# Attention and two feed-forward blocks on one core: conversion temporaries moved to the place of the last value weights, mixes of the second unit moved to the value products, first operations reordered

## The chip, the cores and the metric

The kernel runs on one core of one Trainium2 chip. The metric is device time in microseconds (us) of one execution; the median of the runs counts. Engines are named as the profile names them: PE is TensorE (PEld its weight loads), DVE is VectorE, ACT is ScalarE, POOL is GpSimd, SP issues the DMAs.

## The reference, cut to what matters

Attention with a causal mask and a bias from a running sum, then a block that mixes each row with the row before it, then a gated block. B, H, S, D are 4, 8, 576, 64; the model width is 512, the inner width 1024.

```
def _attn_ref(q, k, v, s):
    scores = q @ k^T / 8
    cum = cumsum(max(s, 0))
    scores = where(causal, -1e9, scores + minimum(-(cum_i - cum_j), 0))
    return softmax(scores) @ v
...
def _moe_ref(x, mu_k, mu_r, w_k, w_v, w_r):
    xk = mu_k * x + (1.0 - mu_k) * x_prev
    xr = mu_r * x + (1.0 - mu_r) * x_prev
    k = np.maximum(xk @ w_k, 0.0)
    v = k * k @ w_v
    r = 1.0 / (1.0 + np.exp(-(xr @ w_r)))
    return r * v
...
def _moe2_ref(x, w_in, g_ln, w_sg, b_sg, w_out):
    h = gelu(x @ w_in); u, v = halves of h
    v_s = w_sg @ layernorm(v) + b_sg
    return x + (u * v_s) @ w_out
```

## The kernel before, in words

**Numbers in two parts.** The weights of the first block are 64-bit words. `load_words` brings 128 x 512 of them (512 KB) by one DMA; `convert` makes two fp32r halves of them: ACT takes an absolute value of the high words (L110), DVE does two scalar operations (L114, L115) and two joins with the words (L116, L117) in a temporary `cvt`, ACT casts it to the first half (L70), DVE subtracts to the second (L73). There are 20 such conversions: 0 to 7 of wk, 8 to 11 of wr, 12 to 19 of wv; `conversions` is a generator that loads AHEAD = 5 ahead. The two temporaries are the halves of one tile `temps`, tag "rt" of the pool `mwork` (L750). A matmul in two parts is three products: high by high, low by high, high by low (`mm3_steps`, L661).

**Attention.** `attend()` is a generator over 20 jobs; each is a pair of heads. Batch 0 has two jobs a pair: jobs 0 to 3 with the row blocks 0 to 2, jobs 4 to 7 with the row blocks 3 and 4. Batches 1 to 3 have one job a pair (jobs 8 to 19, five blocks). Each step issues the scores of a block for one head (L344, from job 6 on L346 and L347), the fold with mask and minimum on DVE (L361), the exponential on ACT (L387), and part of the job before: transposes (L422, L526), values (L426, L430, L511). From job 8 on the reciprocals of the sums go through memory (`reciprocals`, `spread`), and POOL scales the result xt (L492). `prepare` splits the operands of a job (L327 to L333) and, from job 6 on, loads its bias rows from `gate_d`, which is written once at the start (L298).

**First block.** `moe1()` goes through 8 units, halves of a batch (288 rows). A unit has 8 groups of products with wk (f, 12 matmuls each), 4 groups with wr (m, 12 each), 4 groups with wv (m, 24 each): 240 matmuls. The wk groups end in `kh` and `kl`, the wr groups in a tanh into `rt` (L635, tile tag "rt" in `mwork`), the wv groups in a multiplication with rt on DVE (L647). Ahead of a unit stand its 8 mixes, `mix(u, j, c)`: ACT (L594), DVE (L600), a cast on ACT (L70) and a subtraction on POOL (L73, xl). A unit may be mixed only when its attention is done: `need(u)` issues attention steps until `done[0] > u`. For odd units, `late`, the mixes of the next unit are issued beside the wv groups as soon as done allows, else behind them; for even ones, unit 0 among them, `mix(u + 1, 1, m)` stands behind wr group m and `mix(u + 1, 0, m)` behind wv group m.

**Order.** The order of issue is written by hand in the loop from L805 on: after every second matmul of the first block `due` rises by 2 / Q0 (10) while done is at most 1, by 2 / Q1 (6) while it is at most 2, and by 2 / Q2 (8) after that, and one attention step is issued for each whole one. done is 1 after job 3, 2 after job 7, 4 after the scaling of job 11, 6 and 8 after those of jobs 15 and 19. Products of the first block are tied to follow the latest attention matmul on PE (L663). Within that, a scheduler orders each engine's instructions by priority (`tc.cur_priority`; a smaller number goes first: the first operations -100000, attention -1000, conversions -500, mixes -500). A tile of a new pool that lies on the place of closed pools waits until all of these have been used.

**The start.** s is loaded, cut at zero (L264), summed up by a scan (L266) and copied into the operand rows of job 0 (L269 to L272). The rest of the operand rows is filled by memsets (`rest`). POOL makes the identity and the mask (L249 to L260); mask0 is a copy with one corner set (L262, L263). `gt` is made from `cur` and written to `gate_d`. The tiles zer, cum, cur and gt are in the pool `cum`; it is closed at L299, and the pools opened after it (`xtp` with the tiles xt, `w1b` with wv, `mwork` with rt, xf, kh, kl, kf) take up the room behind it. mu is loaded at L304, after that, and mu1 made from it on POOL (L306). 14 matmuls of 512 columns without use warm up PE (L243).

Of the kernel before, what the change touches and what calls it, by code (L numbers as in the profile page):

```python
# [31 lines left out]
WARM = 14  # L32
# [3 lines left out]
L0, GATE = 0, 1  # L36
GC, LC = 0, 2
XT = 0
# [3 lines left out]
PACE = 3  # L42
N0 = 8
# [8 lines left out]
def block_kernel(ctx: ExitStack, tc: tile.TileContext, qkv, vb, s, w_r, w_k, w_v, mu, w_in, w_out, w_sgT, g_ln, b_sg, out):  # L52
# [184 lines left out]
    if WARM:

        ones = cp.tile([P, 512], BF16, name="ones")
        nc.vector.memset(ones, 1.0)  # L240
        pm = ps_m.tile([P, 512], F32, tag="m", name="warm")
        for _ in range(WARM):
            nc.tensor.matmul(pm, ones[:, 0:P], ones, start=True, stop=True)  # L243
# [29 lines left out]
    tc.cur_priority += FIRST - SECOND  # L273
    cur = cp.tile([48, S], F32, name="cur")
# [33 lines left out]
    xtp = ctx.enter_context(tc.tile_pool(name="xtp", bufs=2))  # L308
    w1b = tc.tile_pool(name="w1b", bufs=1)
    w1bp = w1b.__enter__()  # L310
    wv = Weight(w1bp, "wv", w_v)
# [438 lines left out]
    temps = mw.tile([P, 2, 512], F32, tag="rt", name="cvt")  # L750
# [282 lines left out]
```

## Time and profile before

| | |
|---|---|
| median of 3 runs | 714.64 us (714.37 to 714.86) |
| the profiled execution's own time | 712.34 us |
| its span, first to last instruction | 710.5 us |
| mean granted TensorE clock | 0.964 |
| PE busy | 670.2 us (94%) |
| DVE busy | 510.2 us (72%) |
| ACT busy | 407.8 us (57%) |
| POOL busy | 231.4 us (33%) |
| DMA | 67.48 MB, 95 GB/s in the mean |

One execution of the program is recorded. Busy is the time in which an engine executes; idle time of an engine that isn't the bottleneck costs nothing. The granted clock is 1.00 at 2.4 GHz and 0.50 at 1.2 GHz. A row of a timeline has the start, the duration, the engine, the line of the code, the operation with the tile written and those read, the number of merged instructions, and in brackets the engine's idle time before it with what ended it.

### The profile page before, as it was taken

What the parts mean: (1) busy time and instruction counts of PE and PEld (TensorE: products, weight loads), DVE (VectorE), ACT (ScalarE), POOL (GpSimd) and SP (SyncE); (2) the same over time, 40 slices, a digit from 0 to 9 for tenths busy, and PEclk for the clock granted to TensorE, in tenths of its full rate; (3) what the DMA queues carried; (4) which work ended last, traced back from release to release, by engine and by line L of the source; (5) the groups of instructions that cost most, each with busy time, mean ns of one, the idle gap of its engine ahead of it and who ended that gap; (6) DMA issues with size and microseconds to landing.
All of it is one profiled execution on the core that took longest, in us unless ns stands there. A gap on an engine that the chain in (4) does not pass through costs nothing.

```text
span 710.5 us, 12931 instructions
## 1 busy us (share of the span) xinstructions
PE 670.2 (94%) x4594; PEld 630.0 (89%) x4594; DVE 510.2 (72%) x1225; ACT 407.8 (57%) x978; POOL 231.4 (33%) x234
## 2 busy tenths in 40 slices
PE   6879979998999979999989999999999999999998
PEld 3657879987999969998989999999998998998998
DVE  8869998877878688779678598852946664664643
ACT  5759776877988867797777453633433133133120
POOL 7013553546655763576463073030000000000000
PEclk8779976999999999999999999999999999999999
DMA  9884542345244332424200630004230400300101
GB/s 242 238 253 145 155 123 56 95 125 159 73 128 141 89 107 57 143 85 119 89 22 21 204 131 29 6 18 142 78 117 3 131 3 5 129 1 5 63 1 68
DMA packets 39832, 67.48 MB, mean 95 GB/s; under 512 B 6908, under 2 KB 23400, under 8 KB 39736
## 3 DMA queue, kind: packets, MB, share of 16 engines
q1 hardware_dynamic: 39768, 66.66, 31.5%
q8 instruction: 36, 0.59, 0.3%
q14 instruction: 28, 0.23, 0.1%
HBM read 51.85 MB, written 10.19 MB: 87 GB/s over the span
## 4 chain that ended last, share of the span: by engine, by line
PE 71%; ACT 10%; DVE 10%; issue 3%; DMA 3%; POOL 1%; SPq 1%; DVEq 0%; ACTq 0%; POOLq 0%
PE m L661 25%; PE pu L674 7%; PE po L674 7%; PE av L511 3%; PE t L526 3%; PE pg L912 2%; PE pg L913 2%; ACT pr L387 2%; PE pg L911 2%; PE s L346 2%; PE av L430 2%; PE pv L848 2%; PE pv L849 2%; PE pv L850 2%; PE s L347 2%
## 5 line engine op out<-in xcount | busy, mean ns | idle before, releaser
L387 ACT ACTIVATE pr<-pr,nm 128x448 f32<-128x448 f32 (+4 forms) x144 | 85.3, 593 | 19.0 <-DVE nm L361 15.4
L73 POOL TENSOR_TENSOR xl<-xf,xh 128x288 fp32r<-128x288 f32 x64 | 69.0, 1091 | 79.5 <-ACT xh L70 40.5
L661 PE MATMUL m<-xh,wk 128*128 128x288 f32 x512 | 82.6, 300 | 0.0
L661 PE MATMUL m<-kh,wv 128*128 128x288 f32 x512 | 79.8, 297 | 0.0
L361 DVE CUSTOM_DVE_ANT_0 pr<-s,mask 128x288 f32<-128x288 f32 (+4 forms) x144 | 64.0, 454 | 15.6 <-PE t L526 6.4
L661 PEld LDWEIGHTS m<-xh,wk 128*128 128x128 f32 x512 | 73.0, 191 | 0.8
L661 PEld LDWEIGHTS m<-kh,wv 128*128 128x128 f32 x512 | 71.7, 188 | 0.5
L346 PE MATMUL s<-qk 128*128 128x288 f32 (+4 forms) x144 | 47.4, 330 | 12.2 <-DVE nh L361 7.7
L600 DVE SCALAR_TENSOR_TENSOR xf<-xt,mu_sb,xf 128x288 f32<-128x288 f32 x64 | 43.8, 688 | 12.4 <-ACT xf L594 12.2
L70 ACT CAST xh<-xf 128x288 fp32r<-128x288 f32 (+1 forms) x80 | 36.3, 482 | 24.2 <-DVE xf L600 13.5
L530 DVE TENSOR_TENSOR ptl<-t,pth 128x512 fp32r<-128x512 f32 (+1 forms) x72 | 44.1, 617 | 6.3 <-ACT pth L529 5.9
L661 PE MATMUL m<-xl,wk 128*128 128x288 f32 x256 | 48.1, 303 | 0.0
L594 ACT ACTIVATE xf<-xt,mu 128x288 f32<-128x288 f32 x64 | 33.9, 536 | 24.4 <-POOL xl L73 17.8
L529 ACT CAST pth<-t 128x512 fp32r<-128x512 f32 (+1 forms) x72 | 37.8, 532 | 15.6 <-PE t L526 15.0
L73 POOL TENSOR_TENSOR qk<-qld,qk 64x576 fp32r<-64x576 f32 (+1 forms) x28 | 38.9, 1389 | 20.3 <-DVE qk L70 4.3
L347 PE MATMUL s<-qk 128*128 128x288 f32 (+4 forms) x144 | 44.7, 313 | 0.0
L661 PE MATMUL m<-kl,wv 128*128 128x288 f32 x256 | 44.1, 299 | 0.0
L622 ACT ACTIVATE kf<-m 128x288 f32<-128x288 f32 x64 | 25.9, 410 | 30.6 <-PE m L661 28.9
L346 PEld LDWEIGHTS s<-qk 128*128 128x128 f32 x144 | 28.0, 194 | 16.4 <-DVE nh L361 9.1
L661 PE MATMUL m<-xh,wr 128*128 128x288 f32 x256 | 41.0, 301 | 1.3 <-ACT rt L635 1.0
L674 PE MATMUL pu<-xh,wi 128*128 128x288 f32 x256 | 40.6, 295 | 0.2 <-ACT ut L874 0.2
L70 ACT CAST gh<-gf 128x288 fp32r<-128x288 f32 x32 | 13.9, 435 | 46.0 <-DVE gf L918 46.0
(296 smaller groups left out, 1861.4 us busy)
## 6 DMA issues: line engine op xcount, KB each, us to landing
kld<-qkv SPq DMA_DIRECT2D x28, 288.0 KB
qld<-qkv SPq DMA_DIRECT2D x24, 288.0 KB
x_d<-rt SPq DMA_DIRECT2D x8, 576.0 KB
xf<-x_d SPq DMA_DIRECT2D x8, 576.0 KB
outT<-ot SPq DMA_DIRECT2D x32, 144.0 KB
vld<-qkv SPq DMA_DIRECT2D x24, 160.0 KB
qk<-qk SPq DMA_DIRECT2D x24, 144.0 KB
rb<-rd SPq DMA_DIRECT2D x24, 128.0 KB
```

Of the source, the lines that this page charges most:

```text
L70: nc.scalar.copy(dst, src) if eng == "A" else nc.vector.tensor_copy(dst, src)
L73: (nc.gpsimd if pick(engines) == "P" else nc.vector).tensor_tensor(dst, a, b.bitcast(F32), ALU.subtract)
L346: nc.tensor.matmul(dst, qk[0][:, 0, qs], qk[0][:, 1, ks], start=True, stop=False)
L347: issued[0] = nc.tensor.matmul(dst, qk[1][:, 0, qs], qk[1][:, 1, ks], start=False, stop=True)
L361: nc.vector.tensor_tensor_reduce(out=dst, in0=src, in1=msk, scale=-0.125, scalar=first, op0=ALU.add, op1=ALU.min, accum_out=acc)
L387: i = nc.scalar.activation(dst, dst, AF.Exp, bias=nm[:, col : col + 1], scale=-1.0, accum_out=w.sm[:, col : col + 1])
L529: nc.scalar.copy(pth[:, cols], bank[:, 0:o])
L530: nc.vector.tensor_tensor(ptl[:, cols], bank[:, 0:o], pth[:, cols].bitcast(F32), ALU.subtract)
L594: nc.scalar.mul(xf, xp, mu1[:, j, c : c + 1])
L600: nc.vector.scalar_tensor_tensor(xf, xc, mu_sb[:, j, c : c + 1], xf, ALU.mult, ALU.add)
L661: i = nc.tensor.matmul(dst, w(x, c, m), xx[:, c], start=(n + c == 0), stop=(n == 2 and c == w.nk - 1))
L674: nc.tensor.matmul(dst, w(x, c, m), xx[:, c], start=(n + c == 0), stop=(n == 2 and c == w.nk - 1))
```

## The change

- The temporaries of the conversions are a tile in the place (tag) of the last value weight, wv70, in the pool `w1b`; the last two conversions use a tile `more` of the tag "rb" instead. The last value weight is loaded behind conversion 17.
- L0 is 1: unit 0 counts as late, so the mixes of unit 1 are issued beside or behind the wv groups of unit 0.
- `xtp` and `w1b` are opened before the pool `cum`, so only `mwork` lies on its place.
- mu is loaded with the first loads.
- An exponential of one column stands at the beginning of ACT.
- The low memsets of operand 0's middle part are on DVE; the mask is made before the identity, and mask0 after the first operations, at lower priority.
- The work on gt has priority +300 instead of -1000.
- The warm-up is 18 matmuls of 384 columns; its tile is in the pool `const`.

```
-WARM = 14
+WARM = 18
-L0, GATE = 0, 1
+L0, GATE = 1, 1
+GT = 300
...
-    def conversions(parts, temps, loaded=0):
+    def conversions(parts, temps, loaded=0, last=None):
+        n = len(parts) if last is None else len(parts) - 1
         for i in range(loaded, len(parts) + AHEAD):
-            if i < len(parts):
+            if i < n:
                 load_words(*parts[i], after=temps(i - AHEAD - 1) if i > AHEAD else None)
             if i >= AHEAD:
                 convert(*parts[i - AHEAD], temps(i - AHEAD))
+                if i - AHEAD == last:
+                    load_words(*parts[-1])
                 yield
...
-    def rest(x, a, b, eng):
+    def rest(x, a, b, eng, low):
         eng.memset(qk[x][D:, 0, a:b], 8.0)
-        nc.gpsimd.memset(qk[x][D:, 1, a:b], 0.0)
-        nc.gpsimd.memset(qk[x][D : D + 1, 1, a:b], -8.0)
+        low.memset(qk[x][D:, 1, a:b], 0.0)
+        low.memset(qk[x][D : D + 1, 1, a:b], -8.0)
...
     cur_d = dram.tile([48, S], F32, name="cur_d")
+    mu_sb = const.tile([P, 2, 4], F32, name="mu_sb")
+    nc.sync.dma_start(mu_sb, mu)
+    xtp = ctx.enter_context(tc.tile_pool(name="xtp", bufs=2))
+    w1b = tc.tile_pool(name="w1b", bufs=1)
+    w1bp = w1b.__enter__()
+    wv = Weight(w1bp, "wv", w_v)
     cpool = tc.tile_pool(name="cum", bufs=1)
     cp = cpool.__enter__()
...
+    ones = const.tile([P, 384], BF16, name="ones")
+    nc.vector.memset(ones, 1.0)
+    idle = ps_m.tile([P, 512], F32, tag="m", name="warm")
+    for _ in range(WARM):
+        nc.tensor.matmul(idle[:, 0:384], ones[:, 0:P], ones, start=True, stop=True)
+    first = const.tile([P, 1], F32, name="first")
+    nc.scalar.activation(first, ones[:, 0:1], AF.Exp)
...
-    rest(0, S - KN[2], S + KN[2], nc.vector)
-    rest(1, S - KN[2], S + KN[2], nc.vector)
-    ident = const.tile([P, P], F32, name="ident")
-    make_identity(nc, ident)
+    rest(0, S - KN[2], S + KN[2], nc.vector, nc.vector)
     mask = const.tile([P, 2 * MD + P], F32, tag="mask", name="mask")
...
-    mask0 = const.tile([P, P], F32, name="mask0")
-    nc.vector.tensor_copy(mask0, mask[:, MD : MD + P])
-    nc.vector.memset(mask0[D:, 0:D], 8.0 * NEG)
+    ident = const.tile([P, P], F32, name="ident")
+    make_identity(nc, ident)
+    rest(1, S - KN[2], S + KN[2], nc.vector, nc.gpsimd)
...
     tc.cur_priority += FIRST - SECOND
+    mask0 = const.tile([P, P], F32, name="mask0")
+    nc.vector.tensor_copy(mask0, mask[:, MD : MD + P])
+    nc.vector.memset(mask0[D:, 0:D], 8.0 * NEG)
...
-    tc.cur_priority += SECOND - THIRD
+    tc.cur_priority += SECOND + GT
     gt = cp.tile([48, 2, 4, S], F32R, name="gt")
...
     cpool.__exit__(None, None, None)
-    tc.cur_priority += THIRD
-    mu_sb = const.tile([P, 2, 4], F32, name="mu_sb")
-    nc.sync.dma_start(mu_sb, mu)
+    tc.cur_priority -= GT
...
-    temps = mw.tile([P, 2, 512], F32, tag="rt", name="cvt")
+    temps = w1bp.tile([P, 2, 512], F32, tag="wv70", name="cvt")
+    more = ap.tile([P, S], F32, tag="rb", name="cvt")
     def temp(i):
-        return temps[:, i % 2]
+        return temps[:, i % 2] if i < 18 else more[:, 0:512]
     cvs = conversions(
         [(wk, c, n) for n in range(2) for c in range(4)] + [(wr, c, 0) for c in range(4)] + [(wv, c, 0) for c in range(8)],
         temp,
         loaded=AHEAD,
+        last=17,
     )
```

## Rows read from the trace of the kernel before

**Rows 1.** The page: busy time of PE, and its clock in 40 slices

```profile
PE 670.2 (94%) x4594; PEld 630.0 (89%) x4594; DVE 510.2 (72%) x1225; ACT 407.8 (57%) x978; POOL 231.4 (33%) x234
...
PEclk8779976999999999999999999999999999999999
```

**Rows 2.** Stretches: their length, busy us (count) of PE, PEld, DVE, ACT, POOL; clock, DMA

```profile
0.00:54.80 54.80, 40.13 (x175) 28.89 (x175) 43.39 (x139) 35.21 (x101) 18.09 (x50) 0.78 0.88 243
94.40:121.70 27.30, 22.09 (x112) 20.72 (x113) 25.64 (x54) 18.21 (x41) 11.74 (x10) 0.62 0.31 85
94.40:123.65 29.25, 24.04 (x127) 22.67 (x128) 27.27 (x58) 19.68 (x45) 12.62 (x11) 0.65 0.29 79
159.20:223.00 63.80, 61.43 (x450) 58.20 (x450) 51.06 (x133) 52.18 (x138) 37.52 (x31) 1.00 0.40 115
```

**Rows 3.** Timeline of the start (start, duration, engine, line, operation, tiles, idle before)

```profile
5.36 1.28 ACT L270 ACT_TABLE_LOAD   x1 [5.36 <-DVE cum L266]
6.34 1.58 POOL L159 MEMSET qk<- 1x640 f32 x2
7.40 1.10 PE L344 MATMUL s<-qk 128*128 128x320 f32 x4 [0.62 <-POOL qk L159]
8.25 0.30 POOL L252 TENSOR_SCALAR_AFFINE_SELECT mask<-mask 128x128 f32<-128x128 f32 x1
10.98 0.21 DVE L262 COPY mask<-mask 128x128 f32<-128x128 f32 x1
11.11 0.47 DVE L361 CUSTOM_DVE_ANT_0 pr<-s,mask 128x320 f32<-128x320 f32 x1
```

**Rows 4.** Timeline, 36 to 43 us

```profile
36.22 0.43 SPq L304 DMA_DIRECT2D mu_sb<-mu  x1
40.43 0.20 POOL L306 TENSOR_SCALAR mu<-mu_sb 128x8 f32<-128x8 f32 x1 [9.16 <-DMA mu_sb<-mu]
42.23 0.45 PE L440 MATMUL t<-ident,pr 128*128 128x128 f32 x1 [4.08 <-ACT p L424]
```

**Rows 5.** Timeline, 93 to 125 us

```profile
93.70 0.69 PE L661 MATMUL m<-xl,wr 128*128 128x288 f32 x4
121.74 1.24 PE L661 MATMUL m<-xh,wr 128*128 128x288 f32 x8
122.70 0.95 DVE L73 TENSOR_TENSOR wv<-cvt,wv 128x512 fp32r<-128x512 f32 x1 [0.32 <-ACT wv L70]
124.19 0.70 ACT L635 ACTIVATE rt<-m 128x288 f32<-128x288 f32 x2
```

**Rows 6.** The chain that ended last: products in a row (start, us)

```profile
393.48 9.90 PE m L661 x76
```

**Rows 7.** Conversions, 94.4 to 123.65: busy us of DVE, ACT; then min/median/max ns

```profile
94.40:123.65 29.25, 16.84 (x23) 5.28 (x9) 0.65 0.29 79
...
L73 DVE TENSOR_TENSOR wv<-cvt,wv x5: 644/686/1747, 100.7 to 122.7; 128x512 fp32r<-128x512 f32 x5
L115 DVE TENSOR_SCALAR cvt<-cvt x4: 421/425/428, 97.3 to 117.8; 128x512 int32<-128x512 int32 x4
```

**Rows 8.** Timeline of DVE: a mix

```profile
249.61 3.01 DVE L600 SCALAR_TENSOR_TENSOR xf<-xt,mu_sb,xf 128x288 f32<-128x288 f32 x1
```

**Rows 9.** Timeline: two loads and their first users; the gate DMAs, the xt memsets

```profile
3.91 0.43 SPq L101 DMA_DIRECT2D wk10w<-w_k  x1
10.74 0.67 ACT L110 ACTIVATE cvt<-wk10w 128x512 f32<-128x512 f32 x1 [0.75 <-DMA wk10w<-w_k]
13.71 0.97 SPq L298 DMA_DIRECT2D gate_d<-gt x2
21.72 0.31 POOL L716 MEMSET xt<- 128x1 f32 x8 [3.42 <-DMA qk<-cur_d]
```

**Rows 10.** Timeline, change from unit 1 to unit 2

```profile
215.39 1.43 POOL L492 TENSOR_TENSOR xt<-xt,rb 128x576 f32<-128x576 f32 x1 [0.88 <-DMA rb<-rd]
221.56 0.30 PE L661 MATMUL m<-xh,wk 128*128 128x288 f32 x1
```

More of the change, by code (lines that the diff above doesn't have):

```diff
@@ L35 @@
 U0 = 2
-L0, GATE = 0, 1
+L0, GATE = 1, 1
 GC, LC = 0, 2
-XT = 0
 E1, ND, SECOND, THIRD = 2, 2, 5000, 1000
@@ L234, in block_kernel @@
     cur_d = dram.tile([48, S], F32, name="cur_d")
+    mu_sb = const.tile([P, 2, 4], F32, name="mu_sb")
[4 more added lines that the diff above has]
+    wv = Weight(w1bp, "wv", w_v)
     cpool = tc.tile_pool(name="cum", bufs=1)
     cp = cpool.__enter__()
[L237 to L243, printed above, removed]
+    ones = const.tile([P, 384], BF16, name="ones")
[5 more added lines that the diff above has]
+    nc.scalar.activation(first, ones[:, 0:1], AF.Exp)
     zer = cp.tile([48, S], F32, name="zer")
     nc.gpsimd.memset(zer, 0.0)
-    rest(0, S - KN[2], S + KN[2], nc.vector)
-    rest(1, S - KN[2], S + KN[2], nc.vector)
-    ident = const.tile([P, P], F32, name="ident")
-    make_identity(nc, ident)
+    rest(0, S - KN[2], S + KN[2], nc.vector, nc.vector)
     mask = const.tile([P, 2 * MD + P], F32, tag="mask", name="mask")
@@ L281, in block_kernel @@
         for a, b in ((0, S - KN[2]), (S + KN[2], 2 * S)):
-            rest(x, a, b, nc.gpsimd)
+            rest(x, a, b, nc.gpsimd, nc.gpsimd)
     for c in range(max(1, E1), AHEAD):
         load_words(wk, c % 4, c // 4, after=cur)
-    tc.cur_priority += SECOND - THIRD
+    tc.cur_priority += SECOND + GT
     gt = cp.tile([48, 2, 4, S], F32R, name="gt")
@@ L299, in block_kernel @@
     cpool.__exit__(None, None, None)
-    tc.cur_priority += THIRD
-    mu_sb = const.tile([P, 2, 4], F32, name="mu_sb")
-    nc.sync.dma_start(mu_sb, mu)
+    tc.cur_priority -= GT
     mu1 = const.tile([P, 2, 4], F32, name="mu1")
     nc.gpsimd.tensor_scalar(mu1, mu_sb, -1.0, 1.0, ALU.mult, ALU.add)
[L308 to L311, printed above, removed]
     mwork = tc.tile_pool(name="mwork", bufs=1)
@@ L749, in block_kernel @@
     att = attend()
-    temps = mw.tile([P, 2, 512], F32, tag="rt", name="cvt")
-    more = [ap.tile([P, S], F32, tag=t, name="cvt") for t in ("rb",)] if XT else []
+    temps = w1bp.tile([P, 2, 512], F32, tag="wv70", name="cvt")
+    more = ap.tile([P, S], F32, tag="rb", name="cvt")
     def temp(i):
-        if i < XT:
-            return more[0][:, 0:512] if i % 3 == 2 else temps[:, i % 3]
-        return temps[:, i % 2]
+        return temps[:, i % 2] if i < 18 else more[:, 0:512]
     cvs = conversions(
```

## The prediction

> **What bounds the kernel now.** I read the page's first part, then the stretches, then the timeline at each stretch where TensorE loses time. Over the whole span TensorE is the bound: 94% busy, so some 40 us idle in all, and a change can only give back idle time or time at the lower clock [rows 1]. That time is not spread evenly: the string of granted clocks falls below 9 only in the first seven slices, that is before 125 us [rows 1], and from 159 to 223 us TensorE is busy 61.43 of 63.8 us at full clock [rows 2]. Ahead of that, VectorE (DVE) is the bound: busy 43.39 of the first 54.8 us, and 27.27 of the 29.25 us in which the last weight conversions run [rows 2]. So the early part is to be read as a row of DVE work with a few holes, and what counts is how early that row ends and what TensorE finds to do meanwhile.
>
> Three places stand out.
> 1. The start. The first scores begin at 7.40 and the mask is ready at 8.55 (8.25 + 0.30), but the first fold starts at 11.11, behind the copy of mask0 at 10.98 on the in-order DVE [rows 3].
> 2. A hole at 36 to 42 us. The load of mu_sb is issued only at 36.22. POOL idles 9.16 us for it and does the scaling of pr only behind it; ACT and TensorE follow, TensorE having idled 4.08 us [rows 4].
> 3. The stage of the r products of unit 0 (wr; a unit is half a batch). Its first group ends at 94.39; the next begins at 121.74, and its evacuation, the tanh into rt, comes at 124.19, after the last conversion's subtraction (122.70 + 0.95) [rows 5]. Two causes are written in the code: rt and the conversion temporaries have one tag, hence one place, and the mixes of unit 1 ahead of wr group 1 call need(1), which issues the attention up to job 8 in one go, ahead of further wr products.
>
> **The change, part by part.** The sum is made against the profiled execution, 712.34 us (span 710.5); the median shown is 714.64, 2.3 higher, and I carry the difference over to it.
>
> *Start (T1).* On POOL the mask goes ahead of ident; mask0's copy and memset leave the head of the queue; one Exp at the beginning draws the table load (1.28 us at 5.36, on the way to the first scores [rows 3]) into time in which ACT is idle (ACT's first work is at that load); the two low memsets of operand 0 go from POOL to DVE, whose gaps hide them (11.4 us idle before 54.8 [rows 2]); without that cover they cost DVE what they cost POOL, 0.79 us for the row of -8 [rows 3]. If the fold starts when its mask is ready, 11.11 - 8.55 = 2.6 us. Below: 0, if DVE's other early work merely changes places; above 3.9, with the table load counted too. I take 2.6, the row of the mask being the nearest. The warm-up becomes 18 x 384 instead of 14 x 512 columns (6912 for 7168): nothing.
>
> *The hole (T2).* mu_sb is now loaded with the first loads, one issue of 0.43 us on SP; what is queued behind it there are operands of job 1, not needed before the first job is through. POOL's mu1 then no longer stands before pr. I take TensorE's own wait, 4.1 us; 0 if DVE's row swallows it, 5.5 if the lower clock behind the hole goes as well.
>
> *Temporaries and mixes (T3).* In 94.4 to 121.7 TensorE is busy 22.09 us at a mean clock of 0.62 [rows 2]. With the 5.2 idle us at either clock the work is 11.7 to 14.3 us at full clock; I take the middle, 13.0, so 14.3 of 27.3 us are lost. That work is some 8 attention steps (done reaches 2 at step 18, ten to eleven are issued before): 1.6 us each. After the change wr's three other groups no longer wait for rt, nor for the burst: 36 products at 9.90/76 = 0.13 us [rows 6] are 4.7 us, and at one step per ten products 3.6 steps (5.9 us) lie among them: 10.6 us of TensorE work. But DVE still has the conversions, 16.84 us [rows 7], and its other 10.4 us (27.27 - 16.84) shrink only to 3.6/8, 4.7. So 21.5 us pass in which TensorE works 10.6: 10.9 us are still lost, 3.4 us are gained. Beside it, the conversions are longer than they need be: clean, these 23 instructions would take 8 x 0.43 and 15 x 0.69 (the subtraction's median, taken for the joins too), 13.8 us [rows 7]; the excess of 3.0 us comes while POOL subtracts (1.75 instead of 0.69 at worst). About half of POOL's subtractions leave the stretch: 1.5 us. T3 = 4.9; below 0, above 14.3 (all that is lost).
>
> The Trainium skill, page "SBUF — State Buffer", section "Who interferes with whom", says that a DVE instruction with two SBUF inputs contends with a GpSimd instruction that reads SBUF, one blocking the other. The trace agrees: a mix's multiply-add takes 3.01 us at 249.61 [rows 8]. It speaks against the change: the mixes' POOL subtractions don't vanish, they come where folds and the same multiply-adds run. By the rule alone T3 would be 3.4 and the time 707.5.
>
> *Given back (T4).* Without the burst attention is behind. Counting the issues at one step per 10, 6 and 8 products: before, unit 0 ends at step 40 and unit 1 at 80, and done reaches 4 at step 76, just in time for unit 2's mixes. After, done reaches 2 halfway through the second of unit 0's four value groups, unit 0 ends at step 28, unit 1 at 68: 8 steps short, issued in one go before unit 2. In unit 1 a step costs DVE at most 51.06/40 = 1.28 us and TensorE (61.43 - 240 x 0.13)/40 = 0.75 [rows 2, 6], so 8 x 0.53 = 4.2 us would be lost; 0 if attention gets ahead while the value products wait for the conversions; 6.8 at unit 1's pace (8 x 1.6 - 6.0). I take 3.0.
>
> *At nothing.* Mixes of unit 1 beside the value products: done reaches 2 in the second group, 60 products before the end, and attention's matmuls cover them; without that cover, see the slower rival. The gate tile's work (two DVE, two ACT instructions, memsets, two DMAs) gets a later priority; DVE's gaps before 55 us, 11.4 us in all, hide it. The last value weight is loaded only after conversion 17 since the temporaries lie in its place, and the last two conversions share one buffer, rb. The nearest load of this size took from 3.91 to 10.74 until its first use [rows 9]; conversion 18 (2.9 us of DVE) and the attention cover most of that. Behind that load SP holds the operands of jobs 6 to 8, for which prepare would wait. 0 to 3.9 us; I take 0, as it is issued as soon as 17 is done and there is other work.
>
> Sum: 2.6 + 4.1 + 4.9 - 3.0 = 8.6. Profiled 703.7; median 714.64 - 8.6 = **706.0**.
>
> **Rivals.**
> - *The gain is larger*: the r stage fills up and the clock stays, T3 near 14.3, T4 0, T1 2.6, T2 4.1: 693.6. For it: a mean clock of 0.62 there [rows 2]; against: the 16.84 us of conversions that stay.
> - *The wait moves*: the change doesn't do what it says. The cumulative-sum tiles now lie under the working pool, so unit 0's first mix waits until the gate DMAs have read them. Before, the xt tiles lay there, and their first memset came at 21.72, 8.0 us after the issue of those DMAs at 13.71 [rows 9]. Issued later still, they hold ACT as mu did: T2 0, or the late last weight costs as much: 714.64 - 2.6 - 4.9 + 3.0 = 710.1.
> - *Nothing*: DVE's early row absorbs T1 and T2 and T3 equals T4: 714.6.
> - *Slower*: unit 2 waits. Before, the last scaling of batch 1's attention stood at 215.39, and unit 2's first product at 221.56 [rows 10], 6.2 us later and just covered. 8 steps short at unit 1's pace are 8 x 1.6 = 12.8 us; with those 6.2 us then uncovered, less 6.0 us of attention on TensorE, 13.0 us. With T1 and T2 gained and T3 0: 714.64 - 6.7 + 13.0 = 720.9. It decides where the 8 steps cost over 6.7 us more than TensorE has to do.
>
> **How the numbers follow.** Forecast 0.48 (own range 700 to 710), larger gain 0.20, wait moved 0.13, nothing 0.07, slower 0.12. Faster by over 0.2% (what a measurement of this kernel can tell from no change): 0.48 + 0.20 + 0.13 = 0.81; same 0.07; slower 0.12. The range takes in the larger gain with its upper T1 (714.64 - 3.9 - 4.1 - 14.3 = 692.3) and the moved wait with the uncovered late load (710.1 + 3.9 = 714.0), and leaves out the slower case, most of "nothing" and a little at the low end: 692.3 to 714.
>
> **What would show it.** T1: the first fold near 8 us. T2: no idle TensorE of 4 us between 30 and 45, mu1 early. T3: four wr groups close together with their tanh before the last conversion, unit 0's value products some 20 us before 129.9. T4: attention in a row with few products before unit 2's first product. Wrong: a new hole in ACT before the first mix, SP waiting for the last weight, or over 6 us of idle TensorE at the change from unit 1 to 2.

## The result: 717.92 us after 714.86, slower by 0.6%

Median of 11 runs each on the same chip: 717.92 us (715.15 to 721.15) against 714.86 (709.92 to 715.77); the ratio is 1.0064, 95% interval 1.0041 to 1.0087. The forecast was 706.0. The profiled execution took 721.15 us (span 719.4), 3.2 above its median, that of before 712.34, 2.5 below its own: the two traces differ by 8.8 us, more than the medians. Lines of the changed kernel are higher by 4 from the scores on (L661 is L665, L594 is L598); the gate DMAs are L309 instead of L298.

The page of after, to be laid beside [rows 1]:

```profile
PE 673.0 (94%) x4598; PEld 632.0 (88%) x4598; DVE 509.0 (71%) x1226; ACT 406.2 (56%) x979; POOL 230.4 (32%) x232
...
PEclk8879898899998999999999999999999999999999
```

Half of TensorE's busy time at the lower clock comes to 22.3 us before and 22.6 after: that time moved, its sum did not. To see where, I cut both spans at the same marks: the first wk, wr and wv product of unit 0, then the stores `x_d` that end the units. "Lost" is a stretch's idle time of TensorE plus half of its busy time at the lower clock. From a row that is roughly length less busy, plus (1 - clock) x busy; the table lays the times of the lower clock over TensorE's instructions one by one, which differs from the rows by up to 1.6 us in the first stretch and 0.7 behind it. First before, then after, as stretches with the columns of [rows 2]:

```profile
54.80:92.60 37.80, 34.69 (x238) 31.27 (x238) 36.89 (x89) 31.94 (x73) 18.48 (x16) 0.95 0.49 153
92.60:129.90 37.30, 32.09 (x188) 30.36 (x187) 34.08 (x73) 27.73 (x67) 18.21 (x18) 0.73 0.33 89
129.90:159.20 29.30, 27.86 (x201) 26.00 (x200) 23.24 (x63) 21.23 (x54) 14.94 (x16) 1.00 0.37 102
223.00:289.10 66.10, 60.64 (x426) 57.18 (x425) 51.50 (x122) 49.78 (x127) 39.54 (x38) 0.97 0.35 101
397.60:442.10 44.50, 43.50 (x294) 41.08 (x293) 37.93 (x78) 20.93 (x44) 19.31 (x8) 1.00 0.37 124
```

```profile
54.70:95.20 40.50, 36.50 (x235) 32.52 (x234) 40.40 (x91) 32.70 (x77) 17.43 (x18) 0.92 0.41 129
95.20:111.80 16.60, 14.73 (x117) 14.11 (x114) 16.53 (x33) 13.22 (x32) 12.00 (x9) 1.00 0.38 104
111.80:146.80 35.00, 31.32 (x204) 30.25 (x202) 23.40 (x61) 21.39 (x56) 13.29 (x18) 0.85 0.30 84
213.50:289.20 75.70, 66.31 (x451) 61.58 (x450) 59.93 (x141) 57.86 (x150) 45.63 (x44) 0.95 0.37 104
400.80:448.40 47.60, 44.06 (x288) 41.76 (x287) 37.47 (x78) 21.67 (x46) 19.96 (x11) 0.96 0.36 127
```

The same for the runs that carry the argument (length / lost, us; the last line has the exponentials begun on ACT, which stand for the attention steps: nine of them to a job from job 8 on, somewhat fewer than steps):

| stretch | before | after | e1 | e12 | e17 |
|---|---|---|---|---|---|
| to the first wk product | 54.8 / 24.6 | 54.7 / 23.8 | 53.6 / 21.1 | 53.8 / 23.9 | 55.9 / 24.8 |
| unit 0, wk | 37.8 / 4.8 | 40.5 / 7.4 | 42.0 / 9.1 | 37.7 / 3.9 | 38.1 / 4.8 |
| unit 0, wr | 37.3 / 14.1 | 16.7 / 1.9 | 30.7 / 5.7 | 36.1 / 12.3 | 35.5 / 10.8 |
| unit 0, wv | 29.2 / 1.4 | 34.9 / 8.8 | 29.2 / 1.4 | 29.0 / 1.3 | 19.3 / 0.0 |
| unit 1 | 63.9 / 2.4 | 66.7 / 3.8 | 63.7 / 1.1 | 62.2 / 0.8 | 63.1 / 1.4 |
| unit 2 | 66.0 / 7.2 | 75.8 / 12.7 | 62.3 / 4.3 | 61.9 / 3.5 | 71.7 / 8.9 |
| units 3 and 4 | 108.6 / 3.3 | 111.6 / 1.3 | 108.4 / 3.3 | 106.5 / 1.9 | 112.0 / 1.9 |
| unit 5 | 44.4 / 1.0 | 47.6 / 5.2 | 44.5 / 1.0 | 44.4 / 0.9 | 46.6 / 2.7 |
| exponentials by the end of unit 0, 1 | 56, 85 | 48, 76 | 56, 86 | 56, 85 | 50, 76 |

Each column is one execution, and single stages vary between executions of the same instructions. Before, e4, e12 and e17 issue the same up to 91 us; their first product comes at 54.8, 52.5, 53.8 and 55.9. After, e2, e14 (but for two warm-up matmuls) and e16 issue the same up to 132 us; their value stage loses 8.8, 7.0, 6.8 and 2.0. So a difference of 2 us in one stage of two traces shows little, and the medians decide.

Unit 0 ends 12.4 us earlier, with 8 exponentials fewer begun. The r stage gained as meant (14.1 to 1.9). The start gained nothing, and later places took the rest back.

**The hole is still there**, with another owner. Timeline of the start:

```profile
8.54 0.49 DVE L365 CUSTOM_DVE_ANT_0 pr<-s,mask 128x320 f32<-128x320 f32 x1
34.59 0.31 SPq L309 DMA_DIRECT2D gate_d<-gt  x1
39.08 0.53 ACT L598 ACTIVATE xf<-xt,mu 128x288 f32<-128x288 f32 x1 [5.04 <-DMA gate_d<-gt]
40.22 0.69 PE L426 MATMUL t<-ident,pr 128*128 128x128 f32 x2 [4.33 <-ACT pr L391]
54.71 0.77 PE L665 MATMUL m<-xh,wk 128*128 128x288 f32 x4
```

The first fold starts at 8.54 instead of 11.11 [rows 3]; the last gate DMA goes out at 34.59, where both went out from 13.71 on [rows 9], ACT waits 5.04 us for it, TensorE 4.33 instead of 4.08 [rows 4], and the first product comes when it came before.

**The last weight is late.** Timeline, 111 to 126 us:

```profile
111.84 1.06 PE L665 MATMUL m<-kh,wv 128*128 128x288 f32 x6
113.57 0.33 SPq L101 DMA_DIRECT2D wv70w<-w_v  x1
117.98 0.66 ACT L110 ACTIVATE cvt<-wv70w 128x512 f32<-128x512 f32 x1 [2.50 <-DMA wv70w<-w_v]
119.17 0.49 PE L430 MATMUL av<-vb,pth 128*128 128x128 f32 x2 [2.95 <-ACT pth L428]
124.13 1.47 DVE L73 TENSOR_TENSOR wv<-cvt,wv 128x512 fp32r<-128x512 f32 x1 [0.44 <-ACT wv L70]
125.83 2.03 PE L665 MATMUL m<-kh,wv 128*128 128x288 f32 x7
```

The first value product is 18.1 us earlier than at 129.94, but each value group needs all eight weights, and the last is converted at 125.6. Only 4.1 us remain. How much this costs varies: e16, with the same instructions, has its last weight converted at 122.67 and loses 2.0 us in the stage where after lost 8.8:

```profile
112.00:139.90 27.90, 25.88 (x201) 25.19 (x199) 20.57 (x58) 20.68 (x55) 12.55 (x17) 1.00 0.35 98
```

**Unit 2 waits for attention**, to be laid beside [rows 10]:

```profile
213.49 0.54 SPq L658 DMA_DIRECT2D x_d<-rt  x1
222.54 0.70 PE L530 MATMUL t<-ident,pr 128*128 128x128 f32 x3 [1.18 <-DVE xt L563]
226.76 1.43 POOL L496 TENSOR_TENSOR xt<-xt,rb 128x576 f32<-128x576 f32 x1 [4.95 <-DMA rb<-rd]
234.29 1.40 PE L665 MATMUL m<-xh,wk 128*128 128x288 f32 x5
```

Unit 1 is stored at 213.49; the last scaling of batch 1 starts 13.3 us later (before: 7.6 us ahead of the store at 223.02), and products run on from 234.29. Seven more exponentials begin between the store and that scaling.

**Unit 5** loses 3.5 us where two subtractions on POOL take 5.85 us, a mix on ACT waits for them, and a tanh behind it holds TensorE's bank:

```profile
414.06 5.85 POOL L73 TENSOR_TENSOR xl<-xf,xh 128x288 fp32r<-128x288 f32 x2 [9.51 <-ACT xh L70]
420.08 1.77 PE L665 MATMUL m<-xh,wr 128*128 128x288 f32 x8 [3.54 <-ACT rt L639]
```

Unit 5 lost 2.7 to 6.2 us in all eight traces with L0 = 1, and 0.7 to 1.1 in all twelve with L0 = 0. The link (attention ends later beside the units, so these mixes meet the conversions of w_in on DVE) is argued from that, not tried by itself; a subtraction held up by itself is not enough, for in before one takes 7.54 us at 417.87 and the unit loses 1.0.

**Unit 0's wk stage** lost 2.6 us more (7.4 against 4.8). It loses 7.0 to 9.1 in the six traces of the changed kernel with late gate work and 3.1 to 3.5 in e3, e5 and e15 with early gate work, but 10.6 in e11 and 8.1 in e8, so the gate work is not all of it; what waits there was not followed.

### The profile page after: what moved, and what is told of

Read it like the earlier page. It is cut to its first block, busy times and chain, and to the rows that moved or that the text cites. A ratio compares the mean times of both kernels' runs of the same rounds, so it can differ in the third digit from the quotient of the medians.

```text
span 719.4 us, 12943 instructions
## 1 busy us (share of the span) xinstructions
PE 673.0 (94%) x4598; PEld 632.0 (88%) x4598; DVE 509.0 (71%) x1226; ACT 406.2 (56%) x979; POOL 230.4 (32%) x232
## 4 chain that ended last, share of the span: by engine, by line
PE 66%; DVE 12%; ACT 8%; DMA 7%; issue 3%; POOL 2%; SPq 1%; DVEq 0%; POOLq 0%; ACTq 0%
PE m L665 24%; PE po L678 7%; PE pu L678 7%; DVE xf L604 2%; PE av L515 2%; PE t L530 2%; PE pg L916 2%; PE pg L917 2%; PE pg L915 2%; DVE pr L365 2%; PE pv L853 2%; PE pv L852 2%; PE pv L854 2%; PE av L434 2%; ACT pr L391 2%
## 5 line engine op out<-in xcount | busy, mean ns | idle before, releaser
L73 POOL TENSOR_TENSOR xl<-xf,xh 128x288 fp32r<-128x288 f32 x64 | 66.8, 1053 | 104.3 <-ACT xh L70 70.8
L391 ACT ACTIVATE pr<-pr,nm 128x448 f32<-128x448 f32 (+4 forms) x144 | 84.9, 590 | 22.3 <-DVE nm L365 17.5
L665 PE MATMUL m<-xh,wk 128*128 128x288 f32 x512 | 84.3, 302 | 0.2 <-ACT kf L626 0.2
L665 PE MATMUL m<-kh,wv 128*128 128x288 f32 x512 | 79.8, 303 | 0.0
L365 DVE CUSTOM_DVE_ANT_0 pr<-s,mask 128x448 f32<-128x448 f32 (+4 forms) x144 | 64.5, 454 | 21.3 <-PE s L351 13.5
L665 PEld LDWEIGHTS m<-xh,wk 128*128 128x128 f32 x512 | 73.9, 192 | 1.7 <-ACT kf L626 0.5
L665 PEld LDWEIGHTS m<-kh,wv 128*128 128x128 f32 x512 | 72.7, 193 | 0.7
L604 DVE SCALAR_TENSOR_TENSOR xf<-xt,mu_sb,xf 128x288 f32<-128x288 f32 x64 | 49.2, 772 | 15.6 <-ACT xf L598 15.1
L70 ACT CAST xh<-xf 128x288 fp32r<-128x288 f32 (+1 forms) x80 | 36.1, 478 | 24.1 <-DVE xf L604 11.2
L73 POOL TENSOR_TENSOR qk<-qld,qk 64x576 fp32r<-64x576 f32 (+1 forms) x28 | 40.2, 1436 | 27.5 <-DVE qk L70 10.6
L598 ACT ACTIVATE xf<-xt,mu 128x288 f32<-128x288 f32 x64 | 33.6, 534 | 25.1 <-POOL xl L73 17.3
L665 PE MATMUL m<-xl,wk 128*128 128x288 f32 x256 | 47.6, 302 | 0.0
L665 PE MATMUL m<-xh,wr 128*128 128x288 f32 x256 | 43.3, 306 | 3.8 <-ACT rt L639 3.5
L530 PE MATMUL t<-ident,pr 128*128 128x128 f32 x252 | 39.6, 277 | 6.9 <-DVE xt L563 2.9
L665 PE MATMUL m<-kl,wv 128*128 128x288 f32 x256 | 44.0, 300 | 0.0
L665 PEld LDWEIGHTS m<-xh,wr 128*128 128x128 f32 x256 | 37.2, 195 | 4.5 <-ACT rt L639 3.8
L530 PEld LDWEIGHTS t<-ident,pr 128*128 128x128 f32 x252 | 30.1, 141 | 11.7 <-issue 5.4
```

The lines of the kernel that those rows point to most:

```text
L70: nc.scalar.copy(dst, src) if eng == "A" else nc.vector.tensor_copy(dst, src)
L73: (nc.gpsimd if pick(engines) == "P" else nc.vector).tensor_tensor(dst, a, b.bitcast(F32), ALU.subtract)
L365: nc.vector.tensor_tensor_reduce(out=dst, in0=src, in1=msk, scale=-0.125, scalar=first, op0=ALU.add, op1=ALU.min, accum_out=acc)
L391: i = nc.scalar.activation(dst, dst, AF.Exp, bias=nm[:, col : col + 1], scale=-1.0, accum_out=w.sm[:, col : col + 1])
L530: issued[0] = nc.tensor.transpose(bank[:, o : o + P], x, ident)
L604: nc.vector.scalar_tensor_tensor(xf, xc, mu_sb[:, j, c : c + 1], xf, ALU.mult, ALU.add)
```

## The experiments

Each against the kernel before on the same chip: median, ratio, 95% interval.

| run | us | ratio |
|---|---|---|
| after | 717.92 | 1.0064 (1.0041 to 1.0087) |
| e1 after, L0 = 0 | 706.79 | 0.9905 (0.9875 to 0.9935) |
| e2 after, Q1 = 5 | 721.60 | 1.0110 (1.0075 to 1.0145) |
| e3 after, gate early | 711.19 | 0.9963 (0.9932 to 0.9994) |
| e4 before, L0 = 1 | 711.24 | 0.9961 (0.9936 to 0.9985) |
| e5 after, L0 = 0, gate early | 704.78 | 0.9884 (0.9851 to 0.9918) |
| e6 after, last weight earlier | 715.32 | 1.0023 (0.9997 to 1.0049) |
| e7 before, temporaries | 716.00 | 1.0030 (1.0004 to 1.0056) |
| e8 before, mu early | 713.54 | 1.0003 (0.9980 to 1.0027) |
| e9 before, new start | 707.22 | 0.9921 (0.9894 to 0.9948) |
| e10 e5, temporaries on rt | 714.08 | 1.0011 (0.9989 to 1.0032) |
| e11 e5, Q0 = 8 | 708.29 | 0.9933 (0.9905 to 0.9961) |
| e12 before, addition on POOL | 702.76 | 0.9876 (0.9843 to 0.9908) |
| e13 before, 12 warm-ups | 713.04 | 0.9994 (0.9967 to 1.0020) |
| e14 after, 16 warm-ups | 718.96 | 1.0088 (1.0057 to 1.0120) |
| e15 e5, addition on POOL | 703.46 | 0.9877 (0.9849 to 0.9905) |
| e16 after, addition on POOL | 715.66 | 1.0024 (0.9994 to 1.0054) |
| e17 e12, L0 = 1 | 711.96 | 0.9984 (0.9957 to 1.0010) |
| e18 e12, new start, mu early | 704.24 | 0.9866 (0.9830 to 0.9902) |

### Attention owed to unit 2: e1, e2, e4

```
# e1: after
-L0, GATE = 1, 1
+L0, GATE = 0, 1
# e2: after
-Q0, Q1, Q2, MANUAL, LAG = 10, 6, 8, 1, 0
+Q0, Q1, Q2, MANUAL, LAG = 10, 5, 8, 1, 0
# e4: before
-L0, GATE = 0, 1
+L0, GATE = 1, 1
```

> The changed kernel with L0 = 0 again: unit 1's mixes stand behind unit 0's wr groups as before, so need(1) issues attention up to job 8 in one go there; everything else of the change stays. Theory A (attention debt: without that burst attention is 8 steps short, and these are issued in one go before unit 2): TensorE loses under 3 us in 205 to 250, where the changed kernel loses 11.4 (8.0 idle, 3.4 at the lower clock), but the stage of the r products loses its 14 us again instead of 7; about 714. Rival B (the loss of the changed kernel comes from the early wait for the gate DMAs and the late last weight): 717 or more, with the loss in 205 to 250 still above 8.

Measured: 0.9905, 1.6% under the changed kernel. Unit 2 loses 4.3 instead of 12.7, the value products 1.4 instead of 8.8, unit 5 1.0 instead of 5.2; the r stage 5.7, not the 14 that theory A gave it. A holds for unit 2; the burst of attention, once rt is not in its way, is cheaper than thought, and it covers the late weight (issued at 111.24, and no wait of ACT for it). So the changed kernel without L0 = 1 is faster than the kernel before: this one constant turned its sign.

> The changed kernel with Q1 = 5 instead of 6: in unit 1 one attention step per five products, 48 steps instead of 40, so the 8 missing steps are spread over unit 1 and none is left to be issued in one go before unit 2. Theory A (a debt of 8 steps paid in one go costs some 8 us of idle TensorE): 205 to 250 loses under 4 us, time about 709. Rival D (the steps cost the same wherever they are put, since DVE and ACT are full in unit 1 too): the end of unit 1 moves back by what is gained later, 716 to 718.

Measured: 1.0110, no gain; rival D, and worse. Unit 2 loses 3.1 us, but unit 1 7.4 (3.8), unit 3 6.0 (0.2) and unit 5 4.8. The debt can be moved into unit 1; it isn't cheaper there.

> The kernel before with L0 = 1 alone: unit 1's mixes come with unit 0's value products; the temporaries still lie where rt lies, mu is still loaded late, the start is the old one. Theory A: attention is 8 steps short here too; TensorE loses 8 to 13 us in the 45 us around the change from unit 1 to unit 2 (0.3 in the kernel before), and the stage of the r products still waits for rt: about 718. Rival B (the debt does not matter; what costs is the late last weight and the gate wait, which this kernel does not have): 714 or less.

Measured: 0.9961, faster, as rival B gave (714 or less) and against theory A's 718. Unit 2 loses 8.9 us as A says, but 7.2 were lost there before the edit too, by something else. What that was is the matter of e12, and e17 repeats this run without it.

### The two early waits: e3, e5, e8, e9

```
# e3: after; e5: also L0 = 0
-GT = 300
+GT = -1000
# e8: before; the load moves up to the first loads
     cur_d = dram.tile([48, S], F32, name="cur_d")
+    mu_sb = const.tile([P, 2, 4], F32, name="mu_sb")
+    nc.sync.dma_start(mu_sb, mu)
...
-    mu_sb = const.tile([P, 2, 4], F32, name="mu_sb")
-    nc.sync.dma_start(mu_sb, mu)
# e9: before, with all of the change's edits on ones, first, rest, mask, ident and mask0
+    first = const.tile([P, 1], F32, name="first")
+    nc.scalar.activation(first, ones[:, 0:1], AF.Exp)
...
-    rest(0, S - KN[2], S + KN[2], nc.vector)
+    rest(0, S - KN[2], S + KN[2], nc.vector, nc.vector)
```

> The changed kernel with the gate tile's work at priority -1000 as before the change (GT = -1000 instead of 300). Theory B (the first mix waits for the gate DMAs, 5.0 us of ACT, and this holds up TensorE for 4.3 us): gate DMAs issued before 20, first mix before 35, first product of the first block near 50.5 instead of 54.7, time about 714. Rival E (DVE's early row is what counts): the hole goes, but the first product stays above 54, and the time is 717 to 718.

Measured: 0.9963, 1.0% under the changed kernel. The first mix comes at 24.12, the hole is gone, and the first product is at 52.23: later than B's 50.5, yet more time than B gave (52.1 to 52.8 in the four traces with early gate work, 53.1 to 54.7 in the six with late). Behind it the conversions end earlier (the last at 116.4, not 125.6), and unit 0's value stage loses 0.7 instead of 8.8; unit 2 then loses 16.7 instead of 12.7, as it waits for attention all the same.

> The changed kernel with both L0 = 0 and the gate tile's work early (GT = -1000). Theory G (the two are separate losses: the gate wait before the first product, the missing attention before unit 2): the gain of the early gate work, some 5 us, comes on top of that of L0 = 0: first product near 51, about 702. Rival H (what is won at the start is taken by the wait for attention or by DVE later, so the two don't add): first product near 51, but 706 to 708.

Measured: 0.9884, 0.2% under e1, with overlapping intervals: the two don't add, as rival H says, though the time lies below its 706 to 708. As I read it, early gate work is worth much only where the value products have nothing to cover the late weight.

> The kernel before with mu loaded among the first loads and nothing else changed. Theory L (the hole at 36 to 42 us is mu's alone): no idle TensorE of 4 us there, first product near 50.7 instead of 54.8, about 710.5. Rival M (DVE's early row sets the first product): the hole is gone, the first product stays near 54, 713 to 715.

Measured: 1.0003, rival M. The hole is gone; the same stretch in before, then in e8:

```profile
35.00:45.00 10.00, 5.01 (x23) 3.98 (x23) 5.63 (x21) 5.26 (x15) 2.05 (x5) 0.75 0.89 247
```

```profile
35.00:45.00 10.00, 9.38 (x51) 7.26 (x50) 9.11 (x32) 8.06 (x25) 2.31 (x3) 0.87 0.87 241
```

Other waits of TensorE open ahead of it and behind it (timeline of e8):

```profile
31.55 0.55 PE L422 MATMUL t<-ident,pr 128*128 128x128 f32 x3 [2.05 <-ACT pr L387]
47.16 0.72 PE L344 MATMUL s<-qk 128*128 128x288 f32 x2 [1.18 <-DMA qk<-qkv]
```

TensorE works 4.4 us more in that stretch, and the first product comes at 53.59, 1.2 us earlier, which is no more than the spread of traces with before's own instructions (52.5 to 55.9). What sets the start instead (the loads, with a DMA share of 0.79 to 1.04 there, or DVE) was not tried.

> The kernel before with the reordered first operations alone (mask ahead of the identity, mask0 behind the first operations, low memsets of operand 0 on DVE, one early Exp, 18 x 384 warm-up); mu, pools, temporaries and L0 as before. Theory N (the earlier first fold moves everything behind it): first fold near 8.3 instead of 11.1, first product 2 to 3 us earlier, about 712. Rival O (behind the first job the loads and DVE set the pace, so the earlier fold is waited away before the first product): first fold near 8.3, first product within 1 us of 54.8, time within 1 us of the kernel before.

Measured: 0.9921, and neither theory: the first fold is at 9.39, the first product at 55.1, no earlier, and the time 0.8% less. The trace has the gain at the r stage (2.4, of which little is sure: e12 has 1.8 there with before's own instructions), unit 1 (1.3) and unit 2 (2.1).

### The temporaries and the late weight: e6, e7, e10

```
# e6: after
-        return temps[:, i % 2] if i < 18 else more[:, 0:512]
+        return temps[:, i % 2] if i < 16 else more[:, 0:512]
...
-        last=17,
+        last=15,
# e7: before, with the change's conversions() and temp()
-    temps = mw.tile([P, 2, 512], F32, tag="rt", name="cvt")
+    temps = w1bp.tile([P, 2, 512], F32, tag="wv70", name="cvt")
+    more = ap.tile([P, S], F32, tag="rb", name="cvt")
...
+        last=17,
# e10: e5, with before's temp() and no late load
-    temps = w1bp.tile([P, 2, 512], F32, tag="wv70", name="cvt")
-    more = ap.tile([P, S], F32, tag="rb", name="cvt")
+    temps = mw.tile([P, 2, 512], F32, tag="rt", name="cvt")
```

> The changed kernel with the last value weight loaded behind conversion 15 instead of 17; conversions 16 to 19 share the one temporary rb. Theory C (the late last weight stops the value products of unit 0: 8.8 us lost there, with L0 = 0 only 1.4): under 3 us lost in that stage, unit 0 ends near 141 instead of 146.8, time 711 to 712. Rival F (unit 2 waits for attention anyway, so unit 0's gain is lost again there): unit 0 ends as early, but unit 2 loses 4 to 6 us more, 716 to 718.

Measured: 1.0023, 0.4% under the changed kernel. The intervals just overlap. The value stage loses 1.5 us and unit 0 ends at 140.5, as theory C says; but e16, with the late weight, loses 2.0 and ends it at 139.9, so this trace by itself doesn't prove C. Unit 2 then loses 18.5. Of 6.2 us that unit 0 is earlier, 1.9 are left at the end of unit 2: rival F.

> The kernel before with the temporaries alone on the last value weight's place, and that weight loaded late; L0 = 0, mu late, the old start. Theory J (the r products waited for rt, the burst alone is harmless): the stage from the first wr product to the first wv product loses about 6 instead of 14.1 us, and nothing is given back: 706 to 707. Rival K (the conversions and the burst fill DVE there anyway, or the late weight costs as much): 712 to 715.

Measured: 1.0030, rival K, a little over its range. The r stage loses 10.7 instead of 14.1 (12.3 in e12, with before's own instructions), and the value stage 4.0 instead of 1.4, with the last weight issued at 119.28 and converted at 130.9 instead of 123.65.

> As the fastest so far (the changed kernel with L0 = 0 and the gate tile's work early, 0.988 of the kernel before), but the conversion temporaries lie on rt's place again and the last weight is loaded in its turn. Theory P (the decoupled temporaries are worth little where the burst of attention stays, as alone: they gave nothing in the kernel before): within 1.5 us of 704.8, the r stage losing 9 to 11 us either way. Rival Q (they carry the gain): 709 to 712, the r stage losing 14 again.

Measured: 1.0011, 1.3% over e5: rival Q, but for a reason that neither named. With the new pool order the temporaries on rt's place lie on the cumulative-sum tiles too, so the first conversion starts at 21.04 (8.76 in before). The first product then comes at 47.3, the earliest of all, and the r stage loses 27.9 us to the conversions that are left. So it doesn't price the temporaries; it shows what early conversions cost at the start, and that they have to be paid.

### A burst shortened: e11

```
# e11: e5
-Q0, Q1, Q2, MANUAL, LAG = 10, 6, 8, 1, 0
+Q0, Q1, Q2, MANUAL, LAG = 8, 6, 8, 1, 0
```

> The changed kernel with L0 = 0, the gate tile's work early and Q0 = 8 instead of 10: in unit 0 one attention step per eight products, so that fewer steps are left to the burst ahead of unit 1. Theory R (a burst costs idle TensorE in proportion to its steps): the r stage loses 5 to 6 us instead of 9.2, about 702. Rival S (DVE is full until the last conversion, so the steps displace conversions one for one): the stage of the wk products is longer by what the r stage gains, 704 to 706.

Measured: 0.9933, 0.5% over e5. The r stage loses 5.4 instead of 9.2, as R gave, the wk stage 10.6 instead of 3.5: rival S, with more time than its 704 to 706.

### What the kernel before lost in units 1 and 2: e12 to e18

The kernel before, and the two parts that gain nothing in it (e7, e8), have two DVE instructions of 3.65 to 3.85 us in units 1 and 2; in e1, e5 and e9 the longest there takes 2.70. They are among the 12 additions of 1e-9 to the nine columns of sums (`reciprocals`). The line's summary in before (min/median/max ns, first and last start):

```profile
L466 DVE TENSOR_SCALAR sm<-sm x12: 160/586/3843, 135.4 to 378.3; 128x9 f32<-128x9 f32 x12
```

The two longest in the timeline of before, with POOL and TensorE beside the first:

```profile
172.55 1.61 POOL L73 TENSOR_TENSOR qk<-kld,qk 64x576 fp32r<-64x576 f32 x1
173.26 3.65 DVE L466 TENSOR_SCALAR sm<-sm 128x9 f32<-128x9 f32 x1
174.12 1.41 POOL L73 TENSOR_TENSOR kl<-kf,kh 128x576 fp32r<-128x576 f32 x1
175.50 1.39 POOL L492 TENSOR_TENSOR xt<-xt,rb 128x576 f32<-128x576 f32 x1
177.54 0.47 PE L346 MATMUL s<-qk 128*128 128x448 f32 x1 [2.25 <-DVE nh L361]
262.34 3.84 DVE L466 TENSOR_SCALAR sm<-sm 128x9 f32<-128x9 f32 x1
```

An addition of 0.16 us holds DVE for 3.65, until 176.91, when the third POOL instruction in a row ends (176.89); the fold behind it is late, and TensorE idles 2.25 us. In all the 12 take 14.8 us in before, 18.1 in e8, 17.7 in e7, 10.1 in e9, 8.5 in e5. So:

```
# in reciprocals(); e12: before; e15: e5; e16: after; e17: e4; e18: e9 with e8
-        (nc.gpsimd if pick(ENG["ia"]) == "P" else nc.vector).tensor_scalar(w.sm[:, cols], w.sm[:, cols], 1e-9, None, ALU.add)
+        nc.gpsimd.tensor_scalar(w.sm[:, cols], w.sm[:, cols], 1e-9, None, ALU.add)
# e13: before
-WARM = 14
+WARM = 12
# e14: after
-WARM = 18
+WARM = 16
```

> The kernel before with one edit: the addition of 1e-9 to the nine columns of sums ahead of the reciprocals (12 times in the run) is on POOL instead of DVE. Theory U (those additions are held up by a row of POOL instructions, 3.65 us at 173.26 and 3.84 at 262.34, each with 2.2 us of idle TensorE and 1.7 us lost at the lower clock behind the second): no such long addition on DVE, units 1 and 2 lose 5 to 7 us less, about 708. Rival V (another DVE instruction meets the same row of POOL instructions instead, or the reciprocal waits for POOL as long): 713 to 716.

Measured: 0.9876: theory U, and more than it gave. This one line makes the kernel before as fast as anything here. In the traces units 1 and 2 lose 4.3 us instead of 9.6, the 5 to 7 of theory U; units 3 and 4, whose addition of 2.75 us at 355.46 is gone too, are 2.1 us shorter; and the first value product, ahead of the first changed instruction, is 2.4 us earlier, which comes from the two executions and not from the edit. The line's summary in e12:

```profile
L466 POOL TENSOR_SCALAR sm<-sm x12: 241/244/343, 132.8 to 369.2; 128x9 f32<-128x9 f32 x12
```

Units 1 and 2 of e12 as stretches; DVE is busy 46.33 us in unit 1, where it was 51.06 [rows 2]:

```profile
156.50:218.80 62.30, 61.52 (x451) 58.34 (x450) 46.33 (x130) 52.53 (x138) 38.23 (x34) 1.00 0.41 117
218.80:280.70 61.90, 59.92 (x426) 56.86 (x426) 47.19 (x121) 49.82 (x127) 42.47 (x42) 0.97 0.37 108
```

One reading in that expectation is wrong: the lower clock (255.0 to 258.4) lies ahead of the second addition (262.34). It follows 2.85 idle us of TensorE behind the mix of 3.01 us [rows 8], and behind the second addition TensorE only idles. Timeline of before:

```profile
253.06 0.47 PE L346 MATMUL s<-qk 128*128 128x448 f32 x1 [2.85 <-DVE nh L361]
266.90 0.39 PE L511 MATMUL av<-ptl,vv 128*128 128x256 f32 x1 [2.21 <-DVE ptl L530]
```

In e12 no mix is held up either (no DVE instruction over 2 us in units 1 and 2), so part of unit 2's gain belongs to a mix that the edit doesn't touch; that the moved additions freed it is not shown.

The other runs bear U out. Of the twelve kernels with L0 = 0, the four with such additions of over 3.6 us in units 1 and 2 (before, e7, e8, e13) take 0.9994 to 1.0030 of the kernel before. Of the eight without, seven take 0.9866 to 0.9933, and e10 has its loss at the r stage.

> The kernel before with 12 instead of 14 warm-up matmuls, an edit with no work in it that matters. Theory W (a reshuffle of the order alone moves the time by several us, since stalls by DVE meeting POOL come and go): more than 3 us from the kernel before, in either direction, with the difference in units 1 and 2. Rival X (the order is stable; the measured effects of single parts are their own): within 2 us.

> The changed kernel with 16 instead of 18 warm-up matmuls. Theory W: more than 3 us from the changed kernel's 717.9 in either direction. Rival X: within 2 us. In both, if attention owed is the cause of the loss ahead of unit 2, unit 2 still loses 9 us or more, as in every kernel with L0 = 1 and Q1 = 6 so far (8.9 to 18.5).

Measured: 0.9994 and 1.0088, within 0.3% of their kernels: rival X. But for the warm-ups themselves both leave the order of every engine as it was, so theory W's reshuffle did not come about: a shift of the start doesn't move the time, and what another order would do was not tried. The 9-column additions are as long in e13 (3.65 and 3.84 us), and unit 2 loses 12.7 in e14. So e9's 0.8% is no mere shift; as its stages have it, it comes by the order that is left in units 1 and 2, not by the first fold, and e18 tells whether anything else is in it.

> The changed kernel with L0 = 0, the gate tile's work early and the nine-column addition on POOL. Its profile without the last edit shows no addition over 1 us on DVE in units 1 and 2, so theory U expects no gain there: 703 to 706; a loss of more than 2 us would speak for rival V.

> The changed kernel with the nine-column addition on POOL. Theory A (the attention owed to unit 2 is the main loss, and it is another cause): only the one held-up addition of unit 1 (3.64 us at 161.43) goes, unit 2 still loses 9 us or more; 713 to 716. Rival Y (the held-up additions explain both kernels): 703 to 707.

Measured: 0.9877, the same as e5, as expected; and 1.0024, 0.4% under the changed kernel with overlapping intervals, unit 2 still losing 11.6 us. The held-up additions are not the changed kernel's trouble: theory A.

> The kernel before with the nine-column addition on POOL (702.8 by itself) and L0 = 1. Theory A: unit 2 loses 8 to 10 us instead of 3.5, of which the r stage and unit 0's value products give back some 2; 706 to 710. Rival Z (L0 = 1 is a gain, as its run on the kernel before seemed to say): 699 to 702.

Measured: 0.9984, 1.1% (7.7 us) over e12: theory A, with a little more than its 706 to 710. Unit 2 of e17:

```profile
212.00:283.70 71.70, 64.49 (x451) 60.26 (x450) 56.63 (x138) 57.84 (x150) 46.91 (x47) 0.98 0.40 110
```

Unit 2 is 9.8 us longer than e12's, with 28 exponentials begun in it instead of 23. L0 = 1 costs 1.1% on e12, 0.8% on e5 (e3), 1.6% on e1 (the changed kernel). With L0 = 1 the edit of e12 is worth nothing that can be told (e4 0.9961, e17 0.9984). As I read it, stalls of TensorE ahead of a wait for attention cost nothing (e4 still has an addition of 4.15 us, at 155.54 in unit 1, which loses 1.8), so in e4 L0 = 1 brought its own loss and made another harmless, which looked like a gain.

> The kernel before with the nine-column addition on POOL, the reordered start and the early mu. If the reordered start's 0.8% came from the held-up additions alone, nothing is left of it here: 701 to 704. If the start and the early mu have gains of their own as forecast (2.6 and 4.1 us): 696 to 699.

Measured: 0.9866, the same as e12: the new start and the early mu have nothing of their own that these runs can tell. e12, e15 and e18 are 1.2 to 1.3% under the kernel before and 1.9 to 2.0% under the changed one; e12 does so with one line.

## Why the prediction was wrong, step by step

**Start, -2.6: right in its row, wrong in what follows.** The fold came 2.6 us earlier, as worked out. That this reaches the first product was assumed; in after (54.7) and e9 (55.1) it doesn't show. In e18 the first product comes at 51.7, and still the time is that of e12 without the new start. The lower bound of 0 was the value.

**Hole, -4.1: wrong twice.** The rival named the wait that took mu's place, down to the gate DMAs; I gave it 0.13. And without that wait the hole was worth 1.2 us at the first product, no more than the spread, and nothing in time (e8, 1.0003): I took TensorE's idle time as the price, though the bound of 0 stood beside it.

**Temporaries and mixes, -4.9: the r stage mis-sized, the late weight costed at nothing.** The r stage gained 12.2 us (14.1 to 1.9), 2.5 times the term. The cover that I named for the last weight, "conversion 18 and the attention", fell short: in the profiled execution the value stage lost 7.4 us more, against 0 to 3.9 (0.6 more in e16). Net 4.8, the forecast's size by accident. What it left out is that all value groups wait for the last conversion, so 18.1 us at the first value product are 4.1 at the next ones.

**Given back, +3.0: the step that turned the sign.** The count of 8 steps was about right (76 exponentials against 85 at the end of unit 1, and seven more by the last scaling). Their price was taken at unit 1's pace, where products lie beside them. But unit 2 cannot start without them: units 1 and 2 lost 6.9 us more, and with unit 5, whose link is only argued, 11.1, near the slower rival's 13.0 for the same 8 steps. As time, L0 = 1 costs 5.6 us (e3 with e5) and 7.7 (e17 with e12), and 11.4 on e1, where the uncovered late weight is in it. The slower rival had the mechanism and the price; its chance of 0.12 was too small, and its sum too large at 720.9, as it took T3 at 0.

**The POOL rule.** The prediction read one mix of 3.01 us [rows 8] and the Trainium skill's page "SBUF — State Buffer", "Who interferes with whom", as a reason for a smaller T3. The trace agrees with contention, but the price was not in T3. It stood in units 1 and 2 of the kernel before: in that very mix, with 2.85 idle us of TensorE behind it, and in additions of 0.16 us that took up to 3.84. The 12 additions are 14.8 of the 510.2 us that DVE is busy, so far down in a list by busy time. Moving them was worth 1.2% of the kernel, twice what the change costs.

**What would show it:** the first fold, the r groups close together, and the hole in ACT and over 6 us of idle TensorE at unit 2 as signs of a miss all came as written.

## What to carry to other kernels

Work put off is a debt with a due date: count the steps that are missing at the next hard wait, and price them there, without the work that would have lain beside them. A wait that is removed is worth what the next waits leave of it at the first point that all work must pass, seldom its own idle time. And compare the shortest with the longest instruction of every line: one far above its minimum, beside a row of POOL work, may be worth more than a redesign.

## What was not expected of the hardware

An addition on nine columns (0.16 us at its shortest) held DVE for 3.65 us and ended 0.02 us behind the third of three POOL instructions that followed each other without a gap: a DVE instruction can wait for a whole row of them. It is no single case. In the fifteen traces with these additions on DVE, 91 of the 180 take over 0.6 us; POOL is busy for at least 94% of each, and each ends 0.02 to 0.08 us after an instruction of POOL ends. On POOL the same addition took 0.24 us, 0.34 at most. It goes the other way too: a subtraction on POOL, 0.81 us at the median, took 5.10 from 414.06 in after, while DVE worked without a gap through nine instructions from 413.98 to 418.51.

The Trainium skill's page "SBUF — State Buffer", section "Who interferes with whom", gives the ports that the two engines share to the one that issues first, for its whole instruction. The rows agree that the other blocks, and show that here it did not get its turn between POOL's instructions.

After the 2.85 us without work ahead of 253.06, TensorE's clock in before fell to 1.2 GHz (0.50) for a stretch, though it was busy again by then:

```profile
250.10:253.10 3.00, 0.14 (x2) 0.05 (x1) 3.00 (x4) 0.65 (x2) 2.21 (x2) 1.00 0.49 161
255.00:258.40 3.40, 3.40 (x17) 3.40 (x16) 0.97 (x3) 3.35 (x9) 0.87 (x1) 0.50 0.02 5
```

That is 3.40 x 0.5, some 1.7 us on top of the stall. After the 2.25 us ahead of 177.54 the clock stayed at 2.4 GHz (1.00 over all of unit 1 [rows 2]).
